# phi(q) token-major through GpSimd and VectorE, num on sixteen 32x32 tiles, and a new order for batch 0, in a fused attention and MoE kernel

## The chip, the cores and the metric

One core of one Trainium2 chip. The metric is the device time of one execution in microseconds (us), as the median of the runs of a kernel. The span is shorter than the time by about 2 us: it runs from the first to the last instruction in the profile. On one core a run is called slow when it is over 1.5% above the fastest of the same kernel. The kernel before varied from 130.0 to 135.1 us over all jobs, so differences under about 1.5 us between jobs are read from the traces, not from the times.

Names: PE is TensorE (matmul), PEld its weight loads, DVE is VectorE, ACT is ScalarE, POOL is GpSimd. A 32-bit matmul shows as two passes (the 144 matmuls of kv with v are x288 in these traces). A divide is the VectorE product that writes x.

## The reference

```python
# q, k, v: (4 batches, 4 heads, 1088 tokens, 32); S1, S2: (8, 32)
def phi(x):                                   # 64 features of a token
    a = einsum('rd,bhsd->bhsr', S1, x); b = einsum('rd,bhsd->bhsr', S2, x)
    return outer(a, b).reshape(..., 64)
kv  = einsum('bhsf,bhsd->bhfd', phi(k), v);  z = phi(k).sum(tokens)
x   = einsum('bhsf,bhfd->bhsd', phi(q), kv) / (einsum('bhsf,bhf->bhs', phi(q), z) + 1e-6)
# then, over all 4352 tokens, x as (4352, 128):
h   = x @ w_in                                # 128 -> 2048
out = (h * sigmoid(beta * h)) @ w_out         # 2048 -> 128
```

## The kernel before

The MoE part is 68 "waves": a wave is 1024 columns of `x @ w_in` into PSUM, one SiLU on ScalarE, and later the matmuls with w_out. The attention of batch 0 stands in front (the prologue); attention of the others is woven between the waves, and the last waves run alone.

phi(q) was made feature-major. Two "spreads" on TensorE repeat a and b over the 64 features, ScalarE copies one out of PSUM, and VectorE multiplies:

```python
    def ab(a_of=None, b_of=None, pool_b=None):
        ...                                   # for both halves c and both heads m:
                nc.tensor.matmul(out=dst[64*c:64*c+64, m, :32*tn],       # 32x64 tiles
                                 lhsT=sx[rows, :], rhs=qT_of[bb][rows, t0:t0+tn, c, :], ...)
        if a_of is not None:
            nc.scalar.copy(out=ASB[a_of][:, :, :w], in_=aps[:, :, :w])
        ...
                nc.vector.tensor_tensor(out=QP[bb][...], in0=bps[...], in1=ASB[b_of][...], op=MUL)
```

phi(k) was already token-major: a projection (`kps`), a turn on VectorE (`kab`), and products on VectorE (`outer`). The prologue and the waves:

```python
    for h in range(H): outer(0, h, 0, 5)
    kv(0, [1, 2, 3, 4])                       # for each j: 4 matmuls with v, 4 with ones (z)
    for h in range(H): outer(0, h, 5, NJK)
    ...
    kv(0, [5, 6, 7, 8, 0])
    ...
    def slot(group, waves):
        ...
            lag = 3 if todo and todo[0][1] == 0 and todo[0][0] > 0 else 2
            while len(todo) >= lag:
                w2(*todo.pop(0))              # output matmuls of an earlier wave
                lag = 2
            w1()                              # matmuls and SiLU of a new wave
```

## Time and profile before

132.05 us, median of 2 runs (131.86 and 132.24); span 130.2 us.

| part | from, to (us) | what sets it |
|---|---|---|
| prologue | 0 to 21.5 | a serial chain up to the first divide, which gives the first x |
| batch 1, 2, 3 | 21.5 to 101.4 | TensorE, in the first of them VectorE too |
| last 22 waves | 101.4 to 125 | a loop of SiLU and wave matmuls, 1.1 us a wave |
| tail | 125 to 130.2 | last output matmuls, turn, store |

The first line of the page's busy times: microseconds, share of the span and number of instructions of each engine.

```profile
PE 113.1 (87%) x1216; PEld 45.9 (35%) x1216; DVE 71.3 (55%) x142; ACT 79.8 (61%) x92; POOL 11.1 (9%) x24
```

Busy time by stretch of the kernel before. The borders are the starts of the first divides of batches 0, 1 and 2 and of the last divide of batch 3. The columns are: stretch, length, busy time of PE, PEld, DVE, ACT and POOL with counts, granted TensorE clock, DMA share, GB/s.

```profile
21.53:52.07 30.54, 27.36 (x338) 10.01 (x336) 23.84 (x41) 20.23 (x24) 3.80 (x7) 1.00 0.70 144
52.07:77.23 25.16, 23.59 (x275) 8.97 (x274) 17.80 (x33) 18.29 (x22) 0.00 (x0) 1.00 0.15 22
77.23:101.39 24.16, 23.46 (x273) 8.82 (x266) 15.24 (x31) 17.23 (x20) 0.00 (x0) 1.00 0.16 24
101.39:130.20 28.81, 21.11 (x103) 9.66 (x101) 3.29 (x5) 20.50 (x22) 0.00 (x0) 0.99 0.22 32
```

In the second and third stretch TensorE stands still for 1.6 and 0.7 us: it is the limit. In the first it stands for 3.2 us.

The groups of instructions (busy us, mean ns of one, then idle time before them) of the path of phi(q), by shape:

```profile
L369 PE MATMUL aps<-qT,s_165 32*64 32x288 f32 x64 | 8.1, 496 | 1.9 <-DVE qT L315 1.1 <-ACT g L267 0.7
L369 PE MATMUL bps<-qT,s_170 32*64 32x288 f32 x64 | 6.7, 493 | 0.1
L379 ACT COPY asb<-aps 128x576 f32<-128x576 f32 x8 | 5.1, 638 | 5.7 <-PE aps L369 4.6 <-PE bps L369 1.1
L388 DVE TENSOR_TENSOR qp<-bps,asb 128x576 f32<-128x576 f32 x8 | 5.8, 740 | 1.6 <-PE bps L369 0.8 <-ACT g L267 0.8
```

Both spreads together cover 15.7 us of TensorE time, 3.6 in the stretch of batch 2.

The timeline of TensorE in the prologue (start, us, what), where the kv and z passes of batch 0 run:

```profile
12.90 0.44 PE L406 MATMUL kvz<-kp,v 128*32 128x64 f32 x8 [0.82 <-DVE qp L388]
13.08 0.47 PE L406 MATMUL kvz<-kp,ones 128*32 128x64 f32 x8
13.29 0.47 PE L406 MATMUL kvz<-kp,v 128*32 128x64 f32 x8
13.51 0.47 PE L406 MATMUL kvz<-kp,ones 128*32 128x64 f32 x8
```

Eight passes start every 0.21 us; 144 of them take 4.13 us.

### The profile page before, as it was taken

How to read it: one execution, taken by the hardware profiler on the slowest of the kernel's cores; microseconds unless marked ns; L12 is line 12 of the kernel's file. 1: busy time of each engine (PE TensorE's matmuls, PEld its weight loads, DVE VectorE, ACT ScalarE, POOL GpSimd, SP SyncE). 2: the span in 40 equal slices, each digit the busy share in tenths (PEclk: the TensorE clock that was granted, in tenths of full speed). 3: DMA queues.
4: the chain of work that ended last, by engine and by line, in shares of the span. 5: the costliest groups of instructions: out<-in, count | busy, mean ns of one | idle time of the engine just before them, and what ended most of it. 6: DMA issues, size and time to landing. Idle time of an engine off the chain costs nothing.

```text
span 130.2 us, 2977 instructions
## 1 busy us (share of the span) xinstructions
PE 113.1 (87%) x1216; PEld 45.9 (35%) x1216; DVE 71.3 (55%) x142; ACT 79.8 (61%) x92; POOL 11.1 (9%) x24
## 2 busy tenths in 40 slices
PE   5787999887889999999997999999999989888830
PEld 2132933222334342342432332443432333334620
DVE  2579119249799988997367579940737400200210
ACT  1303010876358767477777866687776798888930
POOL 3000399700000000000000000000000000000000
PEclk9999999999999999999999999999999999999998
DMA  3999999999992320031000400500032050031232
GB/s 110 304 187 275 358 353 314 208 249 203 235 210 83 56 30 0 5 54 29 5 0 10 71 5 0 81 0 5 0 49 36 0 80 1 0 58 25 35 48 40
DMA packets 24909, 12.42 MB, mean 95 GB/s; under 512 B 18992, under 2 KB 23104, under 8 KB 24896
## 3 DMA queue, kind: packets, MB, share of 16 engines
q1 hardware_dynamic: 24576, 12.19, 42.1%
q8 instruction: 9, 0.15, 0.5%
q10 hardware_dynamic: 320, 0.04, 0.2%
q14 instruction: 4, 0.03, 0.1%
HBM read 10.00 MB, written 2.23 MB: 94 GB/s over the span
## 4 chain that ended last, share of the span: by engine, by line
PE 49%; DVE 22%; ACT 15%; DMA 5%; issue 5%; SPq 1%; ACTq 0%; DVEq 0%
PE moeout L223 15%; ACT g L267 15%; PE wave L259 13%; PE kvz L406 5%; DMA q<-in_q_dram 5%; PE aps L369 4%; DVE kp L346 4%; PE dps L471 3%; DVE qp L388 3%; PE bps L369 2%; DVE rb L489 2%; DVE xT L516 2%; PE nps L506 2%; PE kps L327 2%; DVE qT L315 2%
## 5 line engine op out<-in xcount | busy, mean ns | idle before, releaser
L267 ACT ACTIVATE g<-wave 128x1024 f16<-128x1024 f32 x68 | 67.8, 1023 | 30.1 <-PE wave L259 29.7
L223 PE MATMUL moeout<-g,woutp 128*128 128x512 f16 (+1 forms) x144 | 40.1, 369 | 3.3 <-ACT g L267 3.1
L259 PE MATMUL wave<-xT,winp 128*128 128x512 f16 (+1 forms) x144 | 40.0, 367 | 0.6 <-ACT g L267 0.4
L223 PEld LDWEIGHTS <-woutp 128*128 128x128 f16 x144 | 11.4, 97 | 24.8 <-issue 18.8
L259 PEld LDWEIGHTS <-winp 128*128 128x128 f16 x144 | 13.8, 97 | 17.3 <-issue 3.4
L388 DVE TENSOR_TENSOR qp<-bps,asb 128x576 f32<-128x576 f32 (+1 forms) x16 | 11.3, 713 | 14.5 <-ACT g L267 8.8
L233 DVE STREAM_TRANSPOSE o_sb<-moeout 128x512 f32<-128x512 f32 (+1 forms) x9 | 6.1, 676 | 21.5 <-PE moeout L223 21.5
L369 PE MATMUL aps<-qT,s_165 32*64 32x288 f32 (+1 forms) x128 | 13.6, 448 | 3.1 <-ACT g L267 2.0
L379 ACT COPY asb<-aps 128x576 f32<-128x576 f32 (+1 forms) x16 | 9.8, 610 | 5.7 <-PE aps L369 4.6
L369 PE MATMUL bps<-qT,s_170 32*64 32x288 f32 (+1 forms) x128 | 12.1, 446 | 0.1
L346 DVE TENSOR_TENSOR kp<-kab 128x576 f32<-128x576 f32 (+2 forms) x20 | 11.6, 620 | 0.0
L406 PE MATMUL kvz<-kp,v 128*32 128x64 f32 (+1 forms) x288 | 9.1, 246 | 1.2 <-DVE qp L388 0.8
L147 PE MATMUL warm<-idle 128*128 128x512 f16 x23 | 7.6, 479 | 1.5 <-DVE hm L159 1.5
L369 PEld LDWEIGHTS aps<-qT,s_165 32*64 32x64 f32 x128 | 4.6, 138 | 10.5 <-ACT g L267 5.3
L406 PEld LDWEIGHTS kvz<-kp,v 128*32 128x32 f32 (+1 forms) x288 | 6.5, 124 | 4.5 <-issue 2.3
L516 DVE TENSOR_TENSOR xT<-nps,rb 128x576 f16<-128x576 f32 (+1 forms) x8 | 5.8, 722 | 1.8 <-PE nps L506 1.4
L190 POOL TENSOR_TENSOR winp<-w_in_sb,beta_bc 128x256 f16<-128x256 f32 x8 | 5.5, 721 | 13.6 <-DMA beta_bc<-in_moe_beta_dram 13.6
L482 DVE STREAM_TRANSPOSE dT<-dps 128x288 f32<-128x288 f32 (+1 forms) x8 | 3.7, 463 | 5.1 <-PE dps L471 5.1
L315 DVE STREAM_TRANSPOSE qT<-q 128x576 f32<-128x576 f32 (+1 forms) x8 | 5.8, 726 | 0.8 <-DMA q<-in_q_dram 0.8
L489 DVE STREAM_TRANSPOSE rb<-rc 128x576 f32<-128x576 f32 (+1 forms) x8 | 6.0, 745 | 0.3
L327 PE MATMUL kps<-kT,sk 64*32 64x288 f32 x64 | 3.9, 482 | 2.3 <-DVE kT L303 2.3
L506 PE MATMUL nps<-qp,nd 64*32 64x288 f32 (+1 forms) x128 | 5.5, 401 | 0.0
(56 smaller groups left out, 60.9 us busy)
## 6 DMA issues: line engine op xcount, KB each, us to landing
v<-in_v_dram SPq DMA_DIRECT2D x16, 144.0 KB, 9.2
k<-in_k_dram SPq DMA_DIRECT2D x3, 544.0 KB, 11.8
q<-in_q_dram SPq DMA_DIRECT2D x3, 544.0 KB, 11.0
out_dram<-o_sb SPq DMA_DIRECT2D x20, 64.0 KB, 2.0
w_in_sb<-in_moe_w_in_dram SPq DMA_DIRECT2D x2, 512.0 KB, 8.7
beta_bc<-in_moe_beta_dram SPq DMA_DIRECT2D x2, 512.0 KB, 9.3
w_out_sb<-in_moe_w_out_dram SPq DMA_DIRECT2D x2, 512.0 KB, 9.8
k<-in_k_dram SPq DMA_DIRECT2D x1, 288.0 KB, 2.8
```

What stands on the lines that cost most here:

```text
L223: nc.tensor.matmul(out=moe["acc"][:, :tw], lhsT=woutp[:, j, :], rhs=g[:, jj, :tw], start=(j == 0), stop=(j == NJ - 1),)
L259: nc.tensor.matmul(out=wv[:, jj * tw : (jj + 1) * tw], lhsT=winp[:, (j0 + jj) * P : (j0 + jj + 1) * P], rhs=xT[:, t0 : t0 + tw], start=Tru ...
L267: nc.scalar.activation(out=g, in_=wv, func=ACTF.Silu)
L315: nc.vector.transpose(out=qT_of[b][:, t0 : t0 + tn].rearrange("p t c s -> p (t c s)"), in_=q_t[b][:, 2 * t0 : 2 * (t0 + tn)].rearrange("p ...
L346: nc.vector.tensor_tensor(out=KP[b][:, h, j0:j1].rearrange("p j (i l) -> p j i l", i=R), in0=bass.AP(tensor=a0.tensor, offset=a0.offset, a ...
L369: nc.tensor.matmul(out=dst[64 * c : 64 * c + 64, m, : 32 * tn], lhsT=sx[rows, :], rhs=qT_of[bb][rows, t0 : t0 + tn, c, :], start=True, sto ...
L379: nc.scalar.copy(out=ASB[a_of][:, :, :w], in_=aps[:, :, :w])
L388: nc.vector.tensor_tensor(out=QP[bb][:, 2 * pr : 2 * pr + 2, 32 * t0 : 32 * t0 + w], in0=bps[:, :, :w], in1=ASB[b_of][:, :, :w], op=MUL,)
L406: nc.tensor.matmul(out=kvz[32 * h : 32 * h + 32, F * which : F * which + F], lhsT=v_t[b][:kr, h, j, :] if which == 0 else ones[:kr, :], rh ...
L489: nc.vector.transpose(out=rb[:, :tn].rearrange("p t c s -> p (t c s)"), in_=bass.AP(tensor=r0.tensor, offset=r0.offset, ap=[list(r0.ap[0]) ...
L506: nc.tensor.matmul(out=nps[32 * h : 32 * h + 32, c, :w], lhsT=ND[b][rows, 32 * h : 32 * h + 32], rhs=QP[b][rows, h, 32 * t0 : 32 * t0 + w] ...
L516: nc.vector.tensor_tensor(out=xT[:, o : o + 2 * w].rearrange("p (t c s) -> p c t s", c=2, s=32), in0=nps[:, :, :w].rearrange("p c (t s) -> ...
```

## The change

Intent: take the spreads of batches 1 to 3 off TensorE, their copies off ScalarE and their products off VectorE. q gets the projection of K, its products go token-major mostly to GpSimd (as do eight of the twelve products of K), VectorE turns them in 32x32 blocks, and den and num read the result (num with contraction over 32 on sixteen tiles). Batch 0 keeps the spreads, but its kv runs between the pieces of the products, z is summed four j wide, and its first divide covers 256 tokens. beta is spread over the partitions by TensorE, not by a 1 MB DMA. The issue order is one string.

The core of the diff, with `...` for what is left out and comments of mine:

```diff
+    def qps(b):
+        t = PS["qps"] = two("qps")
+        project(t, lambda rows, g: qT2[b % 2][rows, QB[g] : QB[g] + NJK, :])
+    def outer(dst, b, src, nm, h, j0=0, j1=NJK, eng=None, nh=1):      # now for K and q
+        (eng or nc.vector).tensor_tensor(out=..., in0=..., in1=..., op=MUL)
+    def turn_qo(b, h):
+        nc.vector.transpose(out=QT[b][:, h]..., in_=QO[b][:, h]...)
+    def num_g(b, tiles):
+        for fc in range(2):
+            for h in range(H):
+                for g in range(4):
+                    rows = slice(32 * g, 32 * g + 32)
+                    nc.tensor.matmul(out=tiles[g // 2][32 * h : 32 * h + 32, g % 2, :JW],
+                                     lhsT=ND[b][rows, fc, 32 * h : 32 * h + 32],
+                                     rhs=QT[b][rows, h, :, fc, :], start=(fc == 0), stop=(fc == 1), ...)
...
-    for h in range(H):
-        outer(0, h, 0, 5)
-    kv(0, [1, 2, 3, 4])
...
+    for n, js in enumerate(([0, 1, 2, 3], [4, 5], [6, 7], [8])):
+        nh = 2 if len(js) == 1 else 1
+        for h in range(0, H, nh):
+            outer(KP, 0, KAB, "kp", h, js[0], js[-1] + 1, nh=nh)
+        zj(0, zp, js[0], js[-1] + 1)
+        if n < 2:
+            kv(0, js)
+        if n == 0:
+            u = [wave2("bps") for _ in range(2)]
+            spread("b", 0, u)
+    kv(0, [6, 7, 8])
...
+    # W: a wave. o/p: product of K/q on GpSimd, O/P: on VectorE. t: turn. d, i, n, x: den, reciprocal, num, divide
+    SEQ = """
+        aB tk1 c1 c0 bB W mB1 mB0 w4 kp1 ka1 w6 W w5 dB W o11 W tq1 qp1 O13 qa1 iB w7 W o10 p10
+        W nB p12 W p13 xB p11 O12 W t12 W W Z1 W W va1 t10 t13 t11 vb1 W np1 nz1 tk2 W d1 W i1
+        n1 x10 W x11 kp2 W ka2 O21 W tq2 W o23 W o20 W qp2 o22 W Z2 W va2 qa2 vb2 p21 W P20 p22
+        ...
+        t32 p33 t33 t30 d3 W i3 n3 x30 x31
+    """
```

## The prediction

> **What bounds the kernel now.** Span 130.2 us (time 132.05). By the chain of waits and the timeline:
> - 0 to 22.3 us, prologue, a serial chain: K products on VectorE 9.15 to 12.15, 144 kv/z passes 12.90 to 17.03, turns, den, reciprocal, divide, first wave matmul at 22.34.
> - 22.3 to 101.5 us: 46 of 68 SiLU waves, TensorE-bound: in the busy times by stretch TensorE has 9.7 to 9.9 of most 10 us after 40 us, ScalarE 5.9 to 7.9. In 52 to 77.5 us (one batch, 16 waves) TensorE has: wave 9.4, output 9.3, phi(q) spreads 3.6, kv/z 1.8, den 1.4, num 1.4, K projection 0.7, turn 0.4. From 30 to 40 us it is 83% busy.
> - 101.5 to 125 us: 22 waves, ScalarE-bound, two in 2.19 us. Tail 5.2.
>
> **What the change does.**
> 1. Batches 1 to 3: the spreads (3.6 us a batch) become one projection like that of K (0.72), TensorE -2.9 us. Twice the turns cost +0.4. Num on sixteen 32x32 tiles has twice the passes on twice the tiles: counted as unchanged (1.4). Net -2.5.
> 2. ScalarE loses 12 of 16 asb copies (0.61 each) and gains beta copies and sixteen small w_out scalings. Slack here.
> 3. VectorE loses twelve 0.71 us products, gains two 0.46 us and four 0.75 us transposes a batch, and gives 8 of 12 K products and 9 of 12 q products to GpSimd. My count: 17 us a batch of some 22. GpSimd: 17 products of 576 columns; from w_out's scaling (256 columns, 604 ns) I estimate 1.4 us each, 24 us in all. The Trainium skill (SBUF — State Buffer, "Who interferes with whom") says that a VectorE instruction with two SBUF inputs and a GpSimd one that reads SBUF block each other; the trace of before hardly shows it.
> 4. Prologue: kv runs between product pieces, z takes 16 wide matmuls for 72 narrow, so kv ends about 0.6 us after the last product, not 4.9; the first divide covers 256 tokens. Against it: four strided K turns. beta comes through TensorE, not a 1 MB broadcast DMA, so w_in scaling need not wait until 15.2. First wave matmul about 18.3: -4 us.
> 5. The order again has 46 waves before the last divide and 22 behind it, so the end stays; the last store on two queues gives 0.5.
>
> **Sum.** First wave 18.3; first stage (16 waves) 29.7 -> 26.5; second 25.5 -> 23; third 24 -> 21.8; then 28.7 -> 28.2. Span about 117.8, less 1 for better filled gaps early: 116.8; time about 118. A batch's chain (project, turn, products, turns, den, reciprocal, num, divide) is near 19 us by the same durations, close to a stage, so waits may eat part.
>
> Predicted 118 us, range 113 to 123. Chances: faster 0.94, same 0.04, slower 0.02.
>
> **Signs.** Right: first wave near 18 us; spread passes down from 128 to 32 for each of a and b; TensorE busy near 103; wave spacing at the end still about 1.1 us; ScalarE busy 78 to 81. Wrong: GpSimd products over 2.2 us with many us of waits on GpSimd; num over 2.5 us a batch; first wave after 20.
>
> **What would make it wrong.** Slower: port conflicts of VectorE and GpSimd, or single-buffered tiles holding a batch's chain longer than 16 waves. Faster: sixteen tiles packing better, or waves filling every stall so that ScalarE's 1.1 us a wave binds before 80 us.

## The result

116.12 us (115.92 and 116.31) against 132.05. The ratio is 0.8782, 95% interval 0.8717 to 0.8847. A ratio here is the mean time of one kernel's fast runs over that of the other's fast runs of the same rounds, so it is not quite the ratio of the medians.

The page's busy times of the changed kernel, then its busy time by stretch with the same kind of borders:

```profile
PE 102.2 (90%) x1171; PEld 46.2 (41%) x1171; DVE 73.8 (65%) x144; ACT 79.1 (69%) x99; POOL 31.1 (27%) x44
```

```profile
17.67:42.36 24.69, 23.40 (x344) 12.31 (x343) 21.87 (x37) 18.86 (x27) 10.20 (x10) 1.00 0.50 122
42.36:63.72 21.36, 20.74 (x261) 9.13 (x260) 17.37 (x29) 16.09 (x17) 8.04 (x7) 1.00 0.33 67
63.72:84.87 21.15, 20.57 (x261) 9.01 (x262) 18.44 (x29) 15.19 (x16) 6.69 (x5) 1.00 0.31 64
84.87:113.90 29.03, 21.68 (x105) 9.83 (x103) 3.35 (x5) 21.44 (x22) 0.00 (x0) 1.00 0.21 32
```

The span fell by 16.3 us: 3.86 before the first x (21.53 to 17.67), 5.85, 3.80 and 3.01 in the three batches, and the end gave 0.22 back. In the three batches the sum of 12.66 us is 9.70 less TensorE busy time (74.41 to 64.71) and 2.96 less standing still (5.45 to 2.49).

The groups that replace those shown of before, in the changed kernel (the sixth is the four products of K left to VectorE):

```profile
L402 PE MATMUL qps<-qT,sk 64*32 64x288 f32 x48 | 2.1, 415 | 0.0
L632 PE MATMUL nps<-qt,nd 32*32 32x288 f32 x192 | 5.2, 412 | 0.0
L440 POOL TENSOR_TENSOR qo<-qab 128x576 f32<-128x576 f32 x9 | 12.3, 1394 | 9.2 <-DVE qab L423 9.2
L440 POOL TENSOR_TENSOR kp<-kab 128x576 f32<-128x576 f32 x8 | 9.5, 1216 | 25.0 <-PE wave L330 13.3 <-DVE kab L423 11.7
L440 DVE TENSOR_TENSOR qo<-qab 128x576 f32<-128x576 f32 x3 | 4.0, 1363 | 0.0
L440 DVE TENSOR_TENSOR kp<-kab 128x576 f32<-128x576 f32 x4 | 4.7, 1169 | 0.0
L451 DVE STREAM_TRANSPOSE qt<-qo 128x576 f32<-128x576 f32 x12 | 8.6, 751 | 0.0
```

The projection of q costs 0.7 us a batch in place of 3.6. Num costs 1.6, 1.95 and 1.6 us a batch, against 1.4 before. A product takes 1.2 to 1.4 us on GpSimd; the three of q left to VectorE take 1.36 us and the four of K 1.17, though such a product of K took 0.74 in the kernel before.

The timeline of the kv passes in the new prologue, and the first x and first wave:

```profile
11.29 0.69 PE L500 MATMUL zp<-kp,ones 128*32 128x256 f32 x8
11.81 0.62 PE L488 MATMUL kvz<-kp,v 128*32 128x64 f32 x32
13.77 0.52 PE L488 MATMUL kvz<-kp,v 128*32 128x64 f32 x24
17.67 0.42 DVE L588 TENSOR_TENSOR xT<-nps,rb 128x256 f16<-128x256 f32 x1
20.43 0.61 PE L330 MATMUL wave<-xT,winp 128*128 128x256 f16 x4
```

kv ends at 14.3 us (before: 17.0), the first x comes 3.9 us earlier, but the first wave matmul stands behind the spreads of batch 0's second half in the program. It starts at 20.43, 2.3 us after the end of that divide (0.05 us before the change), so only 1.9 us earlier than before.

### The profile page after: what moved, and what is told of

Read it like the earlier page. It is cut to its first block, busy times and chain, and to the rows that moved or that the text cites. A ratio compares the mean times of both kernels' runs of the same rounds, so it can differ in the third digit from the quotient of the medians.

```text
span 113.9 us, 2896 instructions
## 1 busy us (share of the span) xinstructions
PE 102.2 (90%) x1171; PEld 46.2 (41%) x1171; DVE 73.8 (65%) x144; ACT 79.1 (69%) x99; POOL 31.1 (27%) x44
## 4 chain that ended last, share of the span: by engine, by line
PE 72%; ACT 15%; DVE 6%; issue 2%; ACTq 0%; DVEq 0%
PE moeout L305 22%; PE wave L330 19%; ACT g L339 15%; PE warm L183 6%; PE nps L632 4%; PE kvz L488 4%; PE dps L618 3%; PE kps L402 3%; PE bps L464 2%; PE qps L402 2%; PE betaps L240 2%; PE aps L464 2%; DVE xT L643 1%; PE ndps L533 1%; PE zp L500 1%
## 5 line engine op out<-in xcount | busy, mean ns | idle before, releaser
L339 ACT ACTIVATE g<-wave 128x1024 f16<-128x1024 f32 x68 | 66.4, 1022 | 18.4 <-PE wave L330 18.4
L305 PEld LDWEIGHTS <-woutp 128*128 128x128 f16 x160 | 14.3, 97 | 24.0 <-issue 16.5
L440 POOL TENSOR_TENSOR kp<-kab 128x576 f32<-128x576 f32 x8 | 9.5, 1216 | 25.0 <-PE wave L330 13.3
L440 POOL TENSOR_TENSOR qo<-qab 128x576 f32<-128x576 f32 x9 | 12.3, 1394 | 9.2 <-DVE qab L423 9.2
L451 DVE STREAM_TRANSPOSE qt<-qo 128x576 f32<-128x576 f32 x12 | 8.6, 751 | 0.0
L440 DVE TENSOR_TENSOR kp<-kab 128x128 f32<-128x128 f32 (+2 forms) x18 | 8.1, 506 | 0.0
L643 DVE TENSOR_TENSOR xT<-nps,rb 128x576 f16<-128x576 f32 x6 | 4.5, 744 | 1.4 <-PE nps L632 1.1
L381 DVE STREAM_TRANSPOSE qT<-q 128x1088 f32<-128x1088 f32 (+2 forms) x5 | 5.3, 1052 | 0.0
L488 PE MATMUL kvz<-kp,v 128*32 128x64 f32 x288 | 5.2, 220 | 0.0
L632 PE MATMUL nps<-qt,nd 32*32 32x288 f32 x192 | 5.2, 412 | 0.0
L265 ACT ACTIVATE woutp<-w_out_sb,rbeta 128x128 f16<-128x128 f32 x16 | 5.1, 392 | 0.0
L488 PEld LDWEIGHTS kvz<-kp,v 128*32 128x32 f32 x288 | 4.5, 110 | 1.5 <-issue 0.8
```

The source lines that it names most:

```text
L305: nc.tensor.matmul(out=moe["acc"][:, :tw], lhsT=woutp[:, j, :], rhs=g[jj], start=(j == 0), stop=(j == NJ - 1),)
L339: nc.scalar.activation(out=g[:, :, :gw], in_=wv[:, :, :gw], func=ACTF.Silu)
L440: (eng or nc.vector).tensor_tensor(out=cut(d0, [[NJK * F, nh]] * (nh > 1) + [[F, jn], [R, R], [1, R]]), in0=cut(a0, hs + [[32, jn], [1, R] ...
L451: nc.vector.transpose(out=QT[b][:, h].rearrange("p j c s -> p (j c s)"), in_=QO[b][:, h].rearrange("p j f -> p (j f)"),)
L488: nc.tensor.matmul(out=KVZ[b][32 * h : 32 * h + 32, :F], lhsT=v_t[b][:, h, j, :], rhs=KP[b][:, h, j, :], start=(j == 0), stop=(j == NJK - ...
L632: nc.tensor.matmul(out=tiles[g // 2][32 * h : 32 * h + 32, g % 2, :JW], lhsT=ND[b][rows, fc, 32 * h : 32 * h + 32], rhs=QT[b][rows, h, :, ...
```

## The experiments

All runs gave a correct result. Where a change is small against the noise between jobs, it is read from the trace: the start of the first divide of batch 0 (it varies from 17.1 to 18.4 us over the runs below), then the distance to the first divide of batches 1, 2 and 3, then to the end of the span. In the four kernels whose middle was not touched (changed, e6, e9, e10) the second and third distance repeat within 0.01 us and the end within 0.1, which makes them a fine instrument; the first repeats within 0.1 but for e10, where it is 0.55 longer.

| run | first x | to batch 1 | to 2 | to 3 | to the end | time, us | ratio to before |
|---|---|---|---|---|---|---|---|
| changed kernel | 17.67 | 24.69 | 21.36 | 20.33 | 29.85 | 116.12 | 0.878 |
| e1 all on VectorE | 17.19 | 26.10 | 21.85 | 21.11 | 29.85 | 118.18 | 0.896 |
| e2 more TensorE | 18.09 | 27.02 | 23.30 | 22.28 | 29.91 | 122.56 | 0.928 |
| e3 more VectorE | 17.12 | 26.82 | 23.07 | 22.59 | 29.91 | 121.89 | 0.921 |
| e4 more ScalarE | 17.16 | 26.50 | 22.13 | 20.46 | 29.75 | 118.41 | 0.898 |
| e6 wave first | 18.41 | 24.78 | 21.36 | 20.33 | 29.82 | 116.77 | 0.888 |
| e7 three waves behind | 17.27 | 23.58 | 21.24 | 20.83 | 26.88 | 112.10 | 0.854 |
| e8 both | 17.69 | 24.52 | 21.24 | 21.11 | 26.84 | 113.29 | 0.859 |
| e9 kv late, z wide | 17.41 | 24.69 | 21.36 | 20.34 | 29.90 | 116.69 | 0.890 |
| e10 no fillers | 17.75 | 25.24 | 21.36 | 20.34 | 29.91 | 116.53 | 0.888 |
| e12 two output banks | 17.46 | 23.59 | 21.23 | 20.84 | 26.18 | 112.21 | 0.855 |

The times are medians of all runs of a kernel, slow ones too; without its one slow run e3 has 121.60, e6 116.52, e7 112.06 and e8 112.79. The ratios use fast runs alone, and the half-widths of their 95% intervals are 0.007 to 0.011. The record's class against the kernel before is "faster" for e5 to e8 and "unclear" for the other runs, though all intervals but that of e11 end below 0.94. Runs e1 to e4 shared one job, e5 to e8 another, e9 to e12 a third.

### Which engine sets the middle: e1 to e4

Theory: TensorE bounds the three batches, so its removed time is the gain. Rival: the shorter chains of the other engines are the gain. Each run loads or unloads one engine by about what the change took from it or gave it.

e1 moves every GpSimd product to VectorE:

```diff
-            for c, e in ((str.lower, nc.gpsimd), (str.upper, nc.vector)):
+            for c, e in ((str.lower, nc.vector), (str.upper, nc.vector)):
```

> The changed kernel with its 17 GpSimd products (8 of K, 9 of q) put on VectorE in the same order. They cost 21.8 us on GpSimd; on VectorE at 0.72 us each 12.3 us, less some 3.7 us that VectorE loses now when its own products wait for GpSimd. VectorE would be busy about 67 of the 68 us from 18 to 86. Theory A (the offload to GpSimd is needed: VectorE would become the limit): 4 to 9 us slower, 120 to 125 us. Theory B (TensorE alone limits these stages, the offload is a convenience): under 2 us slower.

Measured: 118.18 us, 2.7 us more over the three batches. Its two groups of 128x576 products on VectorE:

```profile
L440 DVE TENSOR_TENSOR kp<-kab 128x576 f32<-128x576 f32 x12 | 8.5, 734 | 0.1
L440 DVE TENSOR_TENSOR qo<-qab 128x576 f32<-128x576 f32 x12 | 8.4, 737 | 0.0
```

It fell between the two theories. With no products on GpSimd, one takes 0.73 us on VectorE; beside them it took 1.17 (K, four) and 1.36 (q, three) on average. So 17 products moved to VectorE add 7.0 us of busy time (73.8 to 80.8), not 12, and cost 2.7. The offload to GpSimd is worth about a sixth of the whole gain.

e2 adds TensorE work alone:

```diff
-        project(t, lambda rows, g: qT2[b % 2][rows, QB[g] : QB[g] + NJK, :])
+        for _ in range(5):
+            project(t, lambda rows, g: qT2[b % 2][rows, QB[g] : QB[g] + NJK, :])
```

> The changed kernel, but the q projection of batches 1 to 3 is done five times over into the same tile: 4 x 0.72 = 2.9 us more TensorE time a batch, 8.6 in all, which is what the spreads cost over the projection; VectorE, ScalarE and GpSimd unchanged. Theory A (the middle stages are bound by TensorE, so its removed time is the gain): 7 to 9 us slower, 123 to 125 us. Theory B (the gain comes from the other engines' shorter chains, TensorE has slack): under 4 us slower.

The group of these projections, five times as many as in the changed kernel (2.1 us there):

```profile
L402 PE MATMUL qps<-qT,sk 64*32 64x288 f32 x240 | 8.4, 406 | 0.4 <-DVE qT L381 0.4
```

The added work is thus 8.4 - 2.1 = 6.3 us, not the 8.6 that I had worked out. The three batches grew by 2.33 + 1.94 + 1.95 = 6.2 us: all of it. TensorE time goes into the result one for one. Theory A holds, though the total came below its 7 to 9 us because the added work was smaller.

e3 and e4 add one 128x576 operation before each turn of q products, on VectorE and on ScalarE (one of the two lines each; `scr` is a scratch tile):

```diff
     def turn_qo(b, h):
+        nc.vector.transpose(out=scr, in_=w_in_sb[:, :576])      # e3
+        nc.scalar.copy(out=scr, in_=w_in_sb[:, :576])           # e4
```

> The changed kernel with one more 128x576 transpose (0.75 us) from a constant tile into scratch before each turn of q products: 4 a batch, 3.0 us a batch, 9 us in all on VectorE. Theory A (TensorE-bound, VectorE near but under its limit with 17 to 20 of 21 to 23 us busy a stage): 2 to 5 us slower. Theory B (VectorE's chain sets the stages): 8 to 9 us slower. If VectorE has real slack: under 1 us.

> The changed kernel with one more 128x576 copy (about 0.6 us) on ScalarE at the same four places a batch: 2.4 us a batch, 7.2 us in all, what the asb copies of batches 1 to 3 cost before. Theory A (ScalarE has 5 us of slack a stage): under 2 us slower. Theory B (ScalarE, with 68 waves of 1.02 us, is already the limit in the middle too): 6 to 7 us slower.

The added group in e3, then in e4:

```profile
L451 DVE STREAM_TRANSPOSE scr<-w_in_sb 128x576 f32<-128x576 f32 x12 | 9.0, 748 | 0.0
L451 ACT COPY scr<-w_in_sb 128x576 f32<-128x576 f32 x12 | 8.0, 670 | 0.2
```

Measured: e3 adds 9.0 us of VectorE work and the three batches grow by 6.1 us, two thirds of it, just above the range. e4 adds 8.0 us of ScalarE work (0.67 us each) and they grow by 2.7 us, one third, of which 1.8 in the first. So TensorE is the limit, and VectorE is so close behind that two thirds of any addition (where it was put here) shows. The changed kernel is nearly balanced; that is why undoing one part costs less than the part's own time.

### The prologue: e5, e9, e10, e11

e5 undoes two points for batch 0: z narrow again (one j at a time), and kv issued behind all products.

```diff
-        zj(0, zp, js[0], js[-1] + 1)
-        if n < 2:
-            kv(0, js)
...
-    kv(0, [6, 7, 8])
+    for j in range(1, NJK):
+        kv(0, [j - 1])
+        zj(0, zp, j - 1, j)
+    kv(0, [8])
+    zj(0, zp, 8, 9)
...
-    nc.vector.tensor_reduce(out=kvd0[:, 1], in_=cut(zp, [[0, 2], [1, F], [F, 4]]), ...)
+    nc.vector.tensor_copy(out=kvd0[:, 1], in_=cut(zp, [[0, 2], [1, F]]))
```

> The changed kernel with the new order of batch 0 undone in one point: all K products first, then for each j one kv group and one narrow z group (72 z passes of 64 columns, not 32 wide ones, and nothing of kv between the products). Before, such a block of 144 passes took 4.13 us; now the kv and z passes end 1.5 us after the last product. Theory (prologue is a chain that lies whole on the span): first wave 2.5 to 3.5 us later, total 2.5 to 3.5 us slower. Rival (the first wave now waits for the spreads of the second half of batch 0 and not for x, and later stages absorb a late start): under 1 us slower.

The two fast runs took 118.06 and 118.11 us (ratio 0.901), 2 to 3 us more than the changed kernel. The size is near the theory, but the reason is not. The profile fell in the slow state, so only its order of events is used here; the traces of the fast runs were not kept, so whether their 2 us are what follows is not shown. Its timeline of TensorE:

```profile
11.33 0.32 PE L488 MATMUL kvz<-kp,v 128*32 128x64 f32 x8
11.46 0.29 PE L500 MATMUL zp<-kp,ones 128*32 128x64 f32 x8
13.25 0.29 PE L500 MATMUL zp<-kp,ones 128*32 128x64 f32 x8
14.63 0.62 PE L547 MATMUL dps<-qp,zb 128*32 128x256 f32 x3 [0.23 <-DVE zb L536]
17.43 1.07 PE L547 MATMUL dps<-qp,zb 128*32 128x256 f32 x5 [2.19 <-issue]
```

The same 144 narrow passes that took 4.13 us before take 2.2 here, and end at 13.5, earlier than in the changed kernel. Then TensorE stands still inside den, after its 219th pass, and the profile names nothing that it waited for ("issue"); afterwards it runs at half pace for some us. So narrow z sums are not what made the old block long, and a rival was formed: the pace. Eight passes every 0.21 us before, every 0.11 here.

The Trainium skill (TensorE: Matmul & The Clock Gate, "Part 1: The HAM clock gate") says that the array's clock starts at half rate and is released by some 3.4 us of sustained work. The traces agree with the factor of two. No run here shows the 3.4 us: 4.02 us of fillers, from 1.46 on, did not release the kernel before. The profile's column of granted clock says 1.00 for the old block as well, but there it has no record: the clock records kept with the trace begin with the release, and the column counts the time before as full. The first record, at full clock, begins at 16.81 us in the kernel before, 11.45 in the changed kernel, 9.60 in e5, 12.22 in e10 and 4.15 in e11, and the pace of like passes changes at these times. Where there is a record the column does show half rate: in e5 it reads 0.50 from 16.43 to 23.26, which is the half pace after the stall.

e9 keeps z wide and only issues kv late, so TensorE has no more passes than in the changed kernel.

```diff
-        zj(0, zp, js[0], js[-1] + 1)
-        if n < 2:
-            kv(0, js)
...
-    kv(0, [6, 7, 8])
+    for j0, j1 in ((0, 4), (4, 6), (6, 8), (8, 9)):
+        zj(0, zp, j0, j1)
+        kv(0, range(j0, j1))
```

> The changed kernel with kv of batch 0 issued behind all products, but z kept four j wide, so TensorE has as many instructions as in the changed kernel. The run with narrow z ended its kv and z passes at 13.4 us, earlier than the changed kernel (14.3), and lost its time afterwards: TensorE stood 2.2 us inside den with no releaser in the profile and then ran at half pace. Theory A (that stall comes from the 40 added passes, not from the order): no such stall, kv and z end by 14.3, first wave by 20.6, total within 1.5 us of the changed kernel. Theory B (kv late is what costs): stall or late first wave again, 2 us or more slower.

Measured: no stall, kv and z end at 13.8, first wave at 20.17, span 113.7 us. Theory A holds. The interleaving of kv in program order is worth nothing: the products run on another engine, and kv waits for just the piece that it needs in either order.

e10 takes away the fillers before K's projection and before kv.

```diff
-    keep_warm(3)
     kps(0)
...
-    keep_warm(4)
     KVZ[0] = two("kvz")[:, 0]
```

> The changed kernel without the three filler matmuls before the K projection and the four before kv. Theory A (the new prologue is shorter chiefly because TensorE never rests and its passes reach full pace before kv): kv and z passes, 0.11 us for eight in the changed kernel, run at 0.21 us for eight as in the kernel before, turns, den and num too; first wave 1.5 to 3 us later, total 1.5 to 3 us slower. Theory B (the order and the wide z sums make it): less than 0.7 us slower.

The last fillers and the spread behind the first kv passes in the changed kernel, then the first z passes and that spread in e10:

```profile
9.47 1.89 PE L183 MATMUL warm<-idle 128*128 128x512 f16 x4
12.36 0.69 PE L464 MATMUL bps<-qT,s 32*64 32x256 f32 x16
```

```profile
9.71 1.73 PE L500 MATMUL zp<-kp,ones 128*32 128x256 f32 x7 [0.22 <-DVE kp L440]
12.43 0.69 PE L464 MATMUL bps<-qT,s 32*64 32x256 f32 x16
```

Theory A fell. The first 32 kv passes are slow (10.82 to 12.50 us, 1.68 us where the changed kernel takes 0.62), but from 12.4 us the pace is full, kv ends at 14.36 as before the edit (14.29), and the total is the same within the noise. The two effects cancel: four fillers of 1.89 us are gone, so the z and kv passes start at 9.71 and not at 11.29, and at half pace they are done at the same time.

e11 is the kernel before with six more fillers, order and narrow z as they were.

```diff
-    keep_warm(9)
+    keep_warm(11)
...
     kps(0)
+    keep_warm(1)
...
+    keep_warm(3)
     prep_rbeta_mm = prep_rbeta()
```

> The kernel before with six more filler matmuls: 11 for 9 at the start, one behind the K projection, three before kv; its order and its narrow z sums stay. Theory A (half pace of TensorE made the block of 144 kv and z passes 4.13 us): the block takes 2.0 to 2.6 us, the first wave comes 1.5 to 2.5 us earlier, total 1.5 to 2.5 us less than before. Theory B (the 144 narrow passes cost 4.1 us at any pace): no change.

Its timeline of TensorE:

```profile
11.59 0.32 PE L406 MATMUL kvz<-kp,v 128*32 128x64 f32 x8
11.70 0.32 PE L406 MATMUL kvz<-kp,ones 128*32 128x64 f32 x8
15.77 0.68 PE L471 MATMUL dps<-qp,zb 128*32 128x288 f32 x5 [0.25 <-DVE nd L464]
18.28 0.68 PE L471 MATMUL dps<-qp,zb 128*32 128x288 f32 x3 [1.83 <-issue]
```

Half of the expectation held: eight passes every 0.11 us, and the block takes 2.35 us (11.59 to 13.94) for 4.13, with no change of order. So pace made the old block long: that is shown. That the fillers gave the pace is not. TensorE's clock was released at 4.15 us, during the first nine fillers, which the kernel before has too:

```profile
3.56 1.75 PE L147 MATMUL warm<-idle 128*128 128x512 f16 x6
```

The sixth filler starts at 3.56, so up to the release both kernels give TensorE the same work, and the release at 4.15 and not at 16.81 is not the edit's doing. The first wave came at 21.71 (22.34 before) and no change of the time shows (ratio 1.0045, interval 0.987 to 1.022): TensorE stood still for 1.83 us within den, after its 220th pass. That is the same place as in e5 (219), in another kernel, and it went on within a microsecond of the same time (17.43 and 18.28). The kernel before reached its 219th pass at 19.5 us and the changed kernel at 18.5, and neither stands there. This looks like the next block of TensorE's instructions arriving late while the input loads fill the DMA engines: the page lists an "instruction" queue with 9 packets and 0.15 MB. Nine of its packets, of 16 KB, lie in the span of every kernel but e2, which has more TensorE passes and ten packets, so they are TensorE's. The first ran from 15.20 to 16.14 us in e5 and from 15.94 to 16.93 in e11, and the next pass starts 1.29 and 1.35 us after its end; in the kernel before and the changed kernel the 219th pass starts 1.69 and 1.96 us after the end of that packet, so it would have had nothing to wait for. The times fit, but no run here moved that queue, so this cause is argued, not shown. Whatever it is, in these two kernels what was won ahead of that place was lost at it.

### The first wave: e6

```diff
-    keep_warm(7)
+    PS["a"] = [wave2("aps"), two("aps")]
+    spread("a", 1, PS["a"])
+    keep_warm(3)
...
-        aB tk1 c1 c0 bB W mB1 mB0 w4 ...
+        tk1 c1 c0 W bB mB1 mB0 w4 ...
```

> The changed kernel with the a-spread of batch 0's second half issued before the last warm matmuls (3 of 7 kept) and the first wave issued before the b-spread. My failed step had the first wave at 18.3 us; it came at 20.43 behind these spreads. If TensorE's order was what held it, the first wave comes at about 19.0 and, with 1.6 us of fillers replaced by work that was due anyway, the total falls by 1 to 1.7 us. Rival (VectorE's chain kT, kab, products of batch 1 sets the first stage): first wave earlier, total within 0.5 us.

Measured: the first wave comes 1.39 us after the first x (2.76 in the changed kernel), and the distance to batch 1 is 24.78 against 24.69. It cannot come at once after the first x even here: it starts right after the second divide (19.22 to 19.64 us), at 19.80. The rival holds: the first wave's start is not on the path. What counts is the first x and the work that follows it, in whatever order.

### The end: e7, e8, e12

```diff
-            lag = 3 if todo and todo[0][1] == 0 and todo[0][0] > 0 else 2
+            lag = 4 if todo and todo[0][1] == 0 and todo[0][0] > 0 else 3
             while len(todo) >= lag:
                 w2(*todo.pop(0))
-                lag = 2
+                lag = 3
```

> The changed kernel with the output matmuls of a wave issued three waves behind it, not two. At the end (22 waves, 1.1 us each, SiLU 1.02) the chain is SiLU, output matmuls 0.59, wave matmuls 0.45, SiLU: the wave matmuls stand behind output matmuls that wait for the same SiLU. With one more wave of distance the output matmuls are ready earlier. Theory: spacing falls to 1.03 to 1.05 us, total 1.0 to 1.6 us less. Rival (ScalarE's own overhead makes the 1.1): no change.

112.10 us, ratio 0.8544 (0.8466 to 0.8622), which lies below the whole interval of the changed kernel: the best version, with e12. The SiLUs of the last stage in the changed kernel, then in e7 (timeline of ScalarE; x2 and x8 count instructions that ran without a gap):

```profile
92.95 1.94 ACT L339 ACTIVATE g<-wave 128x1024 f16<-128x1024 f32 x2 [0.26 <-PE wave L330]
95.15 1.94 ACT L339 ACTIVATE g<-wave 128x1024 f16<-128x1024 f32 x2 [0.26 <-PE wave L330]
```

```profile
90.13 7.44 ACT L339 ACTIVATE g<-wave 128x1024 f16<-128x1024 f32 x8 [0.20 <-PE wave L330]
97.77 7.44 ACT L339 ACTIVATE g<-wave 128x1024 f16<-128x1024 f32 x8 [0.20 <-PE wave L330]
```

With two waves of distance ScalarE stops 0.26 us after every second SiLU, because the matmuls of the next wave stand on TensorE behind output matmuls that wait for the SiLU just ended. With three it goes eight in a row. The first takes the 1.02 us of one alone, and the other seven add (7.44 - 1.02) / 7 = 0.92 us each: back to back they overlap. The Trainium skill (ScalarE: Activation LUTs, "What ACT_TABLE_LOAD costs") says that back-to-back activations overlap by about 93 ns; here it is 1.02 - 0.92 = 0.10 us, which agrees. The end shrank by 3.0 us, twice the expectation, and the first batch by 1.1, while the third grew by 0.5.

e8 joins e6 and e7.

> Both edits together. If they act in different stages, their gains add: 2 to 3 us less than the changed kernel, 113 to 114 us.

113.29 us (112.79 without the slow run): the end is that of e7, the first batch loses what e7 won there (24.52). The edits do not add, as e6 had nothing to add.

e12 adds a second output bank for the last blocks, so that no longer distance is needed at a block's start.

```diff
+            if ci in (7, 9):
+                moe["acc"] = one("moeout2")
+            else:
                 moe["acc"] = pso.tile([P, TCH], F32, tag="moeout", name="moeout")
...
-            lag = 3 if todo and todo[0][1] == 0 and todo[0][0] > 0 else 2
+            lag = 4 if todo and todo[0][1] == 0 and 0 < todo[0][0] < 7 else 3
...
-                lag = 2
+                lag = 3
```

> The changed kernel with output matmuls three waves behind, and the last token blocks summed in two banks in turn, so that no extra distance is needed at a block's start. In the run with three waves of distance alone ScalarE went at 0.90 us a wave but stood about 1 us at each of two block starts, and the last 16 output passes took 2.0 us. Expected: those gaps shrink, 1 to 2 us less than that run, 110 to 111 us, the best so far.

112.21 us, no faster than e7 beyond the noise (ratio 0.8549). The trace shows why the expected 1 to 2 us were not there: the gaps at block starts in e7 were 0.20 us each (last fence), not 1 us. I had misread pieces of the chain of waits as gaps of ScalarE. The end is 0.7 us shorter (26.18 against 26.88), which is too little for these rounds.

## Why the prediction was right or wrong

The time lies in the range (118 predicted, 113 to 123; 116.12 measured). It came nearer than its sum: the span was predicted at 116.8 and is 113.9, 2.9 us less, but time and span were taken to lie 1.2 us apart and lie 2.4 apart. That part of the agreement is luck. Point by point:

1. "TensorE-bound" from 22 to 101 us: right. e2 shows it for the changed kernel: 6.3 us of TensorE work added, 6.2 us of time. TensorE busy was predicted near 103 and is 102.2; passes of each spread fell from 128 to 32.
2. "Net -2.5" us a batch of TensorE time: mis-sized. Busy time fell by 2.85 and 2.89 in batches 2 and 3 and by 3.96 in the first stretch. Den and kv became a little cheaper (den 1.34 to 1.18 us a batch), the extra turns cost 0.2 and not 0.4; num rose to 1.6 to 1.95 where 1.4 was counted.
3. "less 1 for better filled gaps": mis-sized. TensorE's standing time fell by 2.96 us. Between first divides the batches took 24.69, 21.36 and, to the last divide, 21.15 us. These two terms together are what I missed: from first x to last divide the middle gained 12.66 us, and the sum, which counted from the first wave, had 8.9 for it (79.2 to 70.3).
4. "First wave matmul about 18.3: -4 us": the failed step. It came at 20.43, past the mark of 20 that I had set as a sign of being wrong. The first x did come 3.86 us earlier; the wave was issued behind two spreads. e6 shows that this cost nothing: moved forward by 1.4 us, it left the distance to batch 1 unchanged. I had made the wave's start the border of the sum where the first x was the right one.
5. The reasons given for the shorter prologue, interleaved kv and wide z sums, fell. e9 shows that the order is worth nothing, e5 that narrow sums take 2.2 us, and e11 that the old block's length was TensorE's half pace; that the half pace lasted that long in the profiled run is in part luck. "kv ends about 0.6 us after the last product" was 1.56. How much of the 3.86 us came from where was not separated; e10 shows that the new fillers are not needed for it. That kv began only at 12.90 in the trace of before, and at 11.59 in e11, has a cause in the traces: its first pass waits for the four loads of v, and the last of them, issued at 5.2 us, landed 7.5 us later in the kernel before (12.65), though the profile names a VectorE product. In e11 the last landed at 9.84, in the changed kernel the four took 3.6 to 4.0 us. So some of the 3.86 us may be a late load and a late clock of the one trace of before; beside the 16 us between the two kernels this is little.
6. GpSimd: the estimate of 1.4 us a product was right (1.22 and 1.39). The Trainium skill (GPSIMD Engine Reference, "3.1 Elementwise — side-by-side cycle accounting") has 2.6 cycles an element; at the 1.2 GHz that the page gives, 576 elements are 1.25 us as an estimate. The conflict named from the skill (SBUF — State Buffer, "Who interferes with whom") is real: 0.73 us alone, 1.17 to 1.36 beside GpSimd. I believed the offload to be necessary (e1: 4 to 9 us); it is worth 2.7.
7. The end was predicted unchanged, and it was (1.1 us a wave). But "ScalarE-bound" was the wrong name for it: e7 shows that ScalarE can go at 0.92, so the bound was the order of two kinds of matmuls on TensorE.

## What to carry to other kernels

Put a known extra load on one engine at a time and see how much of it comes out as time: here TensorE gave all of it, VectorE two thirds and ScalarE one third, which says what the next change is worth better than busy shares do. Choose as borders of a sum the event that later work depends on (the first x), not the first visible use of it. When two engines feed each other in a loop and each works off its program in order, as in the timelines of e7, issue the consumer's matmuls one step later before calling either engine the limit: one step here gave 3 to 4 us.

## What the Trainium skill lacked or had wrong

- TensorE: Matmul & The Clock Gate: it does not say that the clock records can begin only with the first release, so that a view which counts missing time as full reads 1.00 while the passes run at half pace (eight passes in 0.21 us in the kernel before, whose first record begins at 16.81 us; 0.11 in e11, where it begins at 4.15). Compare the pace of like passes.
- The same page, "Wait — 56ns, not 53.3ns?", says that starts of matmuls never come closer than about 25 ns. Here eight 64-column passes on four column tiles start within 0.11 us, 14 ns each; the page's figure does not hold for passes on different tiles.
- Runtime: NRT & Kernel Launch is the page for how an engine gets its instructions. Neither it nor another page has a case of TensorE standing still without a releaser early in a kernel: 2.19 us after 219 passes (e5) and 1.83 us after 220 (e11), while the input loads ran, ending 1.29 and 1.35 us after a packet of the instruction queue. The cause is not shown.
- SBUF — State Buffer, "Who interferes with whom": no page sizes the conflict for a mix. Here a 128x576 product with both inputs in SBUF took 0.73 us alone and 1.17 to 1.36 on average beside GpSimd products.
